# Products of zeros between stretches of 32x32 products, in a delta-rule attention with two MLPs behind it

## The chip, the cores and the metric

The kernel runs on one core of a Trainium2 chip. The metric is device time in microseconds (us); the median of three runs of the kernel before stands below.

## The reference

The reference is a gated delta-rule attention over 32 heads (4 batches of 8) of 768 positions and 48 dimensions, followed by two MLPs over 3072 tokens of 384 channels, each with 2048 hidden channels. Cut to what matters:

```python
k_n = k / (norm(k) + 1e-6)
state = zeros((B, H, D, D))
for t in range(S):
    y[:, :, t] = q[:, :, t] @ state
    v_old = state @ k_n[:, :, t]
    state = state + beta[:, :, t] * outer(k_n[:, :, t], v[:, :, t] - v_old)
x = y.transpose(0, 2, 1, 3).reshape(3072, 384)
h = x @ w_in;  x = (P(h) / Q(h)) @ w_out        # first MLP, a rational function
h = x @ w_in2; out = (h * tanh(softplus(h))) @ w_out2   # second MLP
```

## The kernel before, in words

The attention comes first and takes some 320 us; the MLPs follow. The attention works on 12 chunks of 64 positions (u = 0 to 11), all 32 heads at once, as 16 pairs in two halves (h = 0, 1). `Plan.add` records each operation with an engine, an assumed duration in ns, and the buffers it reads and writes; `Plan.best` tries 800 orders of the list and keeps the one whose planned end is earliest; `Plan.run` then emits the operations in that planned order. So each engine has a fixed queue, and in it the work of several chunks is interleaved.

For each chunk, `prepare` normalizes the keys (GpSimd), transposes keys and queries on TensorE (`kn`, `qn`, the products of line 352), copies them out on ScalarE (`kq`), forms the 64x64 gram matrices (line 367) and masks them on VectorE (`gm`, `lg`, line 376). For every second chunk, `inverse` solves a 32x32 triangular system per head step by step on GpSimd (on VectorE for u = 1 and u = 9); its result, transposed on VectorE at line 464, is `xt`, which two chunks share. `step` is the recurrence. For each half h of a chunk it does on TensorE, with 16 products in each group:

- `ks` (line 511): keys by the state `su`, 64x64 weights, 48 columns, into `c_ps`; VectorE subtracts (`rest`, line 519, into `r`)
- `uu` (line 528): `xt` by the remainder, 32x32 weights, 48 columns; ScalarE copies out `u` (line 535)
- `cross` (line 543): the lower block's correction, 32x32 weights, 48 columns; VectorE subtracts
- `uu` again, for the lower 32 rows, and the copy of `u`
- `s_mm` (line 551): the new state in `s_all`, copied out by ScalarE (line 559), which the next chunk's `ks` reads
- `y_mm` (line 566): the outputs in `y_ps`, 64 columns, copied out by ScalarE (line 575)

All of these are float32, so the trace shows two matmul records for each product: a group of 16 products of one half is x32, both halves are x64.

Beside this the plan holds the conversion of the first MLP's weights: loads on the SP queue, a magnitude on ScalarE (line 667), bit operations on VectorE (lines 672 to 688), a copy on ScalarE (line 698) and a difference on GpSimd (line 703).

`heat` is one product of zeros: a 128x128 tile `zero` with 128 columns of the identity, added to columns of PSUM that no one reads (`y_ps` at first, later columns 384 to 511 of `s_all`). `Plan.run` puts such products where the plan has a gap on TensorE, as many as fill 0.9 of it at 200 ns each, less up to 600 ns of idle time. Sixteen more stand at the start. The MLP phase has none.

Of the kernel before, what the change touches and what calls it, by code (L numbers as in the profile page):

```python
# [45 lines left out]
class Ring:  # L46
# [6 lines left out]
    def add(self, pool, **bufs):  # L53
        for tag, b in bufs.items():
            slots = self.slots.setdefault(tag, [])
            self.n[tag] = len(slots)
            slots.extend((pool, b) for _ in range(b))
# [8 lines left out]
class Plan:  # L66
# [12 lines left out]
        self.read = {}  # L79
        self.names = []  # L80

    def add(self, engine, ns, fn, reads=(), writes=(), more=0, early=0):
        i = len(self.ops)
        need = {self.wrote[b] for b in reads if b in self.wrote}
        for b in writes:
            need.update(self.read.pop(b, ()))
            if b in self.wrote:
                need.add(self.wrote[b])
        for b in reads:
            self.read.setdefault(b, []).append(i)  # L90
        for b in writes:
            self.wrote[b] = i
        self.names.append(tuple(writes))
        self.ops.append((engine, ns, fn, sorted(need), more, early))

    def order(self, bias=None):

        n = len(self.ops)
        tail, then, left = [0] * n, [[] for _ in range(n)], [0] * n
        for i in range(n - 1, -1, -1):  # L100
            engine, ns, fn, need, more, early = self.ops[i]
            tail[i] += ns + more
            left[i] = len(need)
            for j in need:
                then[j].append(i)
                tail[j] = max(tail[j], tail[i] + self.HOP)
        tail = [t - self.ops[i][5] + (bias or {}).get(self.kinds[i], 0) for i, t in enumerate(tail)]
        ready = {}
        for i in range(n):
            if not left[i]:  # L110
                ready.setdefault(self.ops[i][0], []).append((0, i))
        free, at, done = {}, [0] * n, []
        while any(ready.values()):
            best = None
            for engine, queue in ready.items():
                if queue:
                    t = max(free.get(engine, 0), min(r for r, _ in queue))
                    if best is None or t < best[0]:
                        best = (t, engine)
            t, engine = best  # L120
            queue = ready[engine]
            pick = max((x for x in queue if x[0] <= t), key=lambda x: (tail[x[1]], -x[1]))
            queue.remove(pick)
            i = pick[1]
            end = t + self.ops[i][1]
            free[engine] = end
            done.append((t, end, i))
            for j in then[i]:
                left[j] -= 1
                at[j] = max(at[j], end + self.ops[i][4] + (0 if self.ops[j][0] == engine else self.HOP))  # L130
                if not left[j]:
                    ready.setdefault(self.ops[j][0], []).append((at[j], j))
        return done
# [3 lines left out]
    def best(self):  # L137

        def end(order):
            return max(e for _, e, _ in order)  # L140
        self.kinds = [(op[0], names[0].strip("0123456789") if names else "") for op, names in zip(self.ops, self.names)]
        kinds, rng = sorted(set(self.kinds)), random.Random(0)
        bias, order = {}, self.order()
        for _ in range(self.TRIALS):
            trial = dict(bias)
            for k in rng.sample(kinds, rng.choice((1, 2, 4))):
                trial[k] = trial.get(k, 0) + rng.gauss(0, rng.choice((1000, 5000, 20000)))
            other = self.order(trial)
            if end(other) <= end(order):
                bias, order = trial, other  # L150
        return order

    WINDOW, IDLE = 3400, 600

    def run(self, idle, unit):

        last, gaps, used = None, [], False
        for t, end, i in self.best():
            engine, ns, fn = self.ops[i][:3]
            if engine == "PE":  # L160
                if last is not None and t > last:
                    gone = sum(max(0, b - max(a, last - self.WINDOW)) for a, b in gaps[-8:])
                    n = max(0, int((t - last - max(0, self.IDLE - gone)) * 0.9 // unit))
                    for _ in range(n):
                        idle(used)
                    gaps.append((last + n * unit, t))
                last, used = end, used or "y_ps" in self.names[i]
            fn()


class Attention:
# [311 lines left out]
    def step(self, p, u):  # L483
# [5 lines left out]
        gm, gmb = self.gm[u % self.NT], f"gm{u % self.NT}"  # L489
        v, vb = self.v[u % self.NV], f"v{u % self.NV}"  # L490
# [4 lines left out]
        i = self.side(u)  # L495
        xt, xb = self.xt[i], f"xt{i}"
        r2, y_ps = self.r2, self.y_ps
        yst, yb = self.yst[0], "yst"

        def each(h):  # L500
            for n in range(W):
                for a in range(2):
                    yield n, a, 64 * (a ^ h), slice(64 * a, 64 * a + 64)

        def out(h, rows, n):
            return self.c_ps[h][rows, n * D:(n + 1) * D]

        def ks(h):
            def f():
                for n, a, r, rows in each(h):  # L510
                    nc.tensor.matmul(  # L511
                        out=out(h, rows, n), lhsT=kq[r:r + 64, 0, n, rows],
                        rhs=S[r:r + 64, h, n, :], start=True, stop=True,
                    )
            return f

        def rest(h, src):
            part = slice(W * h, W * h + W)
            return lambda: nc.vector.tensor_tensor(
                out=r2[:, part], in0=src[:, part],  # L520
                in1=self.c_ps[h][:, 0:W * D].rearrange("p (m d) -> p m d", m=W), op=ALU.subtract,
            )

        def uu(h, c):
            def f():
                for n, a, r, rows in each(h):
                    rows = slice(64 * a + HC * c, 64 * a + HC * c + HC)
                    nc.tensor.matmul(  # L528
                        out=out(h, rows, n), lhsT=xt[rows, u % 2 * M + W * h + n, :], rhs=(r2 if u or c else v)[rows, W * h + n, :],
                        start=True, stop=True,  # L530
                    )
            return f

        def u_out(h):
            return lambda: nc.scalar.copy(
                out=U[:, W * h:W * h + W].rearrange("p m d -> p (m d)"), in_=self.c_ps[h][:, 0:W * D]
            )

        def cross(h):
            def f():  # L540
                for n, a, r, rows in each(h):
                    src, dst = slice(64 * a, 64 * a + HC), slice(64 * a + HC, 64 * a + C)
                    nc.tensor.matmul(
                        out=out(h, dst, n), lhsT=gm[src, W * h + n, 0:HC], rhs=U[src, W * h + n, :], start=True, stop=True,
                    )
            return f
# [32 lines left out]
        def y_add(h, part):  # L579
            need = [f"{ub}{h}", f"{gmb}{2 * h}", f"{gmb}{2 * h + 1}"] if part else [f"{sb}{h}", f"{kqb}1{0}", f"{kqb}1{1}"]  # L580
            if u or part:
                p.add("PE", 1080, y_mm(h, part), need, ["y_ps"])

        p.add("SP", LOAD, lambda: self.load_v(v, u), (), [vb], more=1800)
        for h in range(2):
            c, s, r, uh = f"c{h}", f"{sb}{h}", f"r{h}", f"{ub}{h}"
            if h:
                y_add(1, 0)
            if u:
                p.add("PE", 900, ks(h), [f"{kqb}00", f"{kqb}01", s], [c])  # L590
                p.add("DVE", 560, rest(h, v), [c, vb], [r])
            p.add("PE", 860, uu(h, 0), [r if u else vb, xb], [c])
            p.add("ACT", 480, u_out(h), [c], [uh])
            p.add("PE", 860, cross(h), [f"{gmb}{2 * h}", f"{gmb}{2 * h + 1}", uh], [c])
            p.add("DVE", 560, rest(h, r2 if u else v), [c] if u else [c, vb], [r])
            p.add("PE", 860, uu(h, 1), [r, xb, "y_ps"] if h else [r, xb], [c])
            p.add("ACT", 480, u_out(h), [c], [uh])
        if u + 1 < self.NU:
            for h in range(2):
# [361 lines left out]
def tile_delta_attention_two_mlps(  # L961
# [120 lines left out]
    with ExitStack() as bctx:  # L1082
# [24 lines left out]
        for i in range(n2 + max(LG.values())):  # L1107
# [8 lines left out]
            for op in LISTS[kind]:  # L1116
# [5 lines left out]
                elif op[0] == "u" and i < n2:  # L1122
                    if i not in ups:
                        ups[i] = mlp(i).up(i, *units[i])
                    n = int(op[1])
                    run(ups[i][3 * n:3 * n + 3])
                elif op[0] in "dvy" and 0 <= i - LAG - (op[0] == "y") < n2:
                    j = i - LAG - (op[0] == "y")
# [59 lines left out]
```

## Time and profile before

| | |
|---|---|
| median of 3 runs | 1160.14 us (1158.69 to 1165.7) |
| the profiled execution | 1162.92 us, of which the span from first to last instruction is 1161.2 us |
| attention | from the start to about 321.9 us of the span |
| TensorE busy | 1085.8 us, 94% of the span |
| mean granted TensorE clock | 0.960 of full speed |

The granted clock is a share of 2.4 GHz: 1.00 is 2.4 GHz and 0.50 is 1.2 GHz. In a timeline, the columns are the start, the time to the end of the piece, engine, line, operation and tiles with the shape of the weights and of the columns, how many, and in brackets the idle time of the engine before it with what ended it. "issue" there means that the engine waited for nothing that the profile shows. In a table of windows, "(x...)" is the number of records.

### The profile page before, as it was taken

To read this page: it belongs to the slowest core of one execution; us is meant where nothing else is said; L and a number is where in the kernel's file an instruction comes from. 1 tells how busy PE (TensorE), PEld (TensorE's weight loads), DVE (VectorE), ACT (ScalarE), POOL (GpSimd) and SP (SyncE) were. 2 spreads that over 40 slices of the span, in tenths; PEclk is the share of its full clock that TensorE was granted. 3 is DMA by queue.
4 is the path that set the end of the run, shared out by engine and by line. 5 is a ranking of instruction groups with operands and counts; after the bars stand their busy time and mean duration, and the time that the engine had idled before them with its cause. 6 is when DMAs were issued, how large, how long until landed. Compare 5 with 4: busy or idle time off the path is not lost.

```text
span 1161.2 us, 25029 instructions
## 1 busy us (share of the span) xinstructions
PE 1085.8 (94%) x10354; PEld 945.9 (81%) x10354; DVE 722.5 (62%) x1214; ACT 612.1 (53%) x1093; POOL 532.8 (46%) x607
## 2 busy tenths in 40 slices
PE   5989999878869898999999999999999999999998
PEld 4888888778858777877778778679999999999997
DVE  5976574995658999899898999886121221212110
ACT  4425445323468787888888888754332223333322
POOL 3187877477247676677777767783000000000000
PEclk9998798988889998999999999999999999999999
DMA  7437576226693020120212022161100001010000
GB/s 142 82 83 191 139 209 143 80 58 193 180 351 125 21 96 21 48 68 21 76 41 75 21 69 89 34 210 57 55 1 23 33 1 55 1 55 1 28 1 28
DMA packets 122418, 92.95 MB, mean 80 GB/s; under 512 B 79936, under 2 KB 106688, under 8 KB 122304
## 3 DMA queue, kind: packets, MB, share of 16 engines
q1 hardware_dynamic: 122048, 91.25, 26.9%
q8 instruction: 81, 1.33, 0.5%
q14 instruction: 33, 0.27, 0.1%
q0 software_dynamic: 256, 0.10, 0.1%
HBM read 63.02 MB, written 28.31 MB: 79 GB/s over the span
## 4 chain that ended last, share of the span: by engine, by line
PE 50%; DVE 14%; POOL 14%; ACT 13%; issue 8%; DMA 1%; POOLq 0%; DVEq 0%; ACTq 0%; SPq 0%
PE h L831 19%; PE o L950 17%; POOL q L874 8%; ACT r L881 3%; POOL r L864 3%; ACT q L861 2%; PE c_ps L528 2%; POOL gh L846 2%; ACT r L883 2%; PE y_ps L566 2%; PE c_ps L511 2%; PE o L917 2%; PE s_all L551 2%; DVE tmp L451 2%; DVE gm L376 1%
## 5 line engine op out<-in xcount | busy, mean ns | idle before, releaser
L831 PE MATMUL h<-x,w 128*128 128x512 f32 x1728 | 436.0, 397 | 23.5 <-DVE s L890 13.1
L831 PEld LDWEIGHTS h<-x,w 128*128 128x128 f32 x1728 | 324.3, 190 | 97.6 <-DVE s L890 27.5
L846 DVE TENSOR_TENSOR gh<-g,gh 128x512 fp32r<-128x512 f32 x88 | 63.3, 720 | 286.8 <-ACT g L941 286.8
L950 PE MATMUL o<-w,gh 128*128 128x384 f32 x1152 | 217.5, 337 | 2.0 <-ACT ev L1039 2.0
L917 PE MATMUL o<-gh,w 128*128 128x512 f32 x864 | 214.3, 392 | 0.4 <-ACT ev L1039 0.3
L950 PEld LDWEIGHTS o<-w,gh 128*128 128x128 f32 x1152 | 204.5, 188 | 10.8 <-ACT ev L1039 2.7
L917 PEld LDWEIGHTS o<-gh,w 128*128 128x128 f32 x864 | 163.3, 189 | 36.3 <-ACT ev L1039 2.1
L936 ACT ACTIVATE gh<-h 128x512 fp32r<-128x512 f32 x96 | 57.6, 600 | 215.0 <-PE h L831 215.0
L874 POOL TENSOR_TENSOR q<-q,r 128x512 f32<-128x512 f32 x96 | 127.5, 1328 | 81.6 <-ACT r L868 77.1
L846 POOL TENSOR_TENSOR gh<-g,gh 128x512 fp32r<-128x512 f32 x104 | 136.9, 1316 | 10.9 <-ACT g L941 6.9
L881 ACT ACTIVATE r<-q,cst 128x512 f32<-128x512 f32 x96 | 66.4, 692 | 60.5 <-POOL q L874 60.5
L703 POOL TENSOR_TENSOR w<-wm,w 128x384 fp32r<-128x384 f32 x48 | 48.9, 1020 | 74.7 <-ACT w L698 74.0
L897 DVE SCALAR_TENSOR_TENSOR q<-q,r 128x512 f32<-128x512 f32 x96 | 65.6, 683 | 27.7 <-ACT r L883 27.1
L870 ACT ACTIVATE s<-h,ab 128x512 f32<-128x512 f32 x96 | 74.4, 775 | 0.0
L890 DVE SCALAR_TENSOR_TENSOR s<-s,ab,h 128x512 f32<-128x512 f32 x96 | 71.8, 748 | 3.4
L901 DVE SCALAR_TENSOR_TENSOR r<-s,ab,r 128x512 f32<-128x512 f32 x96 | 71.8, 748 | 0.0
L888 DVE TENSOR_TENSOR s<-s,h 128x512 f32<-128x512 f32 x96 | 65.4, 681 | 9.9 <-ACT s L870 9.9
L906 DVE SCALAR_TENSOR_TENSOR g<-q,r 128x512 f32<-128x512 f32 x96 | 65.9, 687 | 3.3
L457 POOL TENSOR_TENSOR xs<-xs,tmp 128x30 f32<-128x30 f32 (+14 forms) x120 | 62.3, 519 | 9.4
L861 ACT ACTIVATE q<-h 128x512 f32<-128x512 f32 x96 | 57.2, 595 | 13.2 <-PE h L831 13.2
L864 POOL TENSOR_SCALAR r<-q,ab 128x512 f32<-128x512 f32 x54 | 43.4, 803 | 42.6 <-ACT q L861 42.6
L451 POOL TENSOR_TENSOR tmp<-xs 128x30 f32<-128x30 f32 (+14 forms) x120 | 58.6, 488 | 7.0
(125 smaller groups left out, 1403.7 us busy)
## 6 DMA issues: line engine op xcount, KB each, us to landing
w<-w SPq DMA_DIRECT2D x28, 768.0 KB, 7.5
w<-in_moe_w_in_dram SPq DMA_DIRECT2D x32, 384.0 KB, 3.8
w<-in_moe_w_out_dram SPq DMA_DIRECT2D x32, 384.0 KB, 3.5
xraw<-x SPq DMA_DIRECT2D x36, 256.0 KB, 3.9
kn<-in_k_dram SPq DMA_DIRECT2D x48, 96.0 KB, 3.4
qn<-in_q_dram SPq DMA_DIRECT2D x48, 96.0 KB, 3.2
v<-in_v_dram SPq DMA_DIRECT2D x48, 96.0 KB, 3.2
x<-yst SPq DMA_DIRECT2D x24, 192.0 KB, 3.8
```

The costliest lines, as they stand in the source:

```text
L451: eng.tensor_tensor(out=tv, in0=ls[:, j, j + 1:HC].unsqueeze(1).to_broadcast([128, j, n]), in1=xs[:, 0:j, j:j + 1].to_broadcast([128, j, n ...
L831: self.nc.tensor.matmul(out=self.st[i]["h"], lhsT=self.w.t[f][:, a, 0, k], rhs=self.x[g][:, b, k], start=(n == 0), stop=(n == 8),)
L846: (nc.gpsimd if engine == "P" else nc.vector).tensor_tensor(out=s["gh"][:, 1], in0=s["g"], in1=s["gh"][:, 0].bitcast(F32), op=ALU.subtract)
L861: nc.scalar.activation(out=s["q"], in_=s["h"], func=ACTF.Abs)
L864: nc.gpsimd.tensor_scalar(out=s["r"], in0=s["q"], scalar1=k["b1"], scalar2=k["b0"], op0=ALU.mult, op1=ALU.add)
L870: nc.scalar.activation(out=s["s"], in_=s["h"], func=ACTF.Identity, scale=k["a3"], bias=k["a2"])
L874: nc.gpsimd.tensor_tensor(out=s["q"], in0=s["q"], in1=s["r"], op=ALU.mult)
L881: nc.scalar.activation(out=s["r"], in_=s["q"], func=ACTF.Ln, bias=k["c"])
L890: nc.vector.scalar_tensor_tensor(out=s["s"], in0=s["s"], scalar=k["a1"], in1=s["h"], op0=ALU.add, op1=ALU.mult)
L901: nc.vector.scalar_tensor_tensor(out=s["r"], in0=s["s"], scalar=k["a0"], in1=s["r"], op0=ALU.add, op1=ALU.mult)
L917: self.nc.tensor.matmul(out=self.acc[g][d], lhsT=self.w.t[f][:, a, 1, d], rhs=self.st[i]["gh"][:, b], start=(first and n == 0), stop=(last ...
L950: self.nc.tensor.matmul(out=self.acc[g][t][:, 0:384], lhsT=self.st[i]["gh"][:, a, t * 128:(t + 1) * 128], rhs=self.w.t[f][:, b, 1].rearran ...
```

## The change

`Plan.add` gets a flag `small`, which is set on the operations `uu` and `cross`. `Plan.run` now keeps a list `work` of the last TensorE operations with a weight: 0.4 for a small one, 1.0 for any other and for the products of zeros. Before every TensorE operation, whether the plan has a gap there or not, it sums the weighted work of the plan's last 3400 ns (over the last 16 entries) and adds up to three products of zeros, as many 200 ns products as are missing to 0.7 of that time.

```diff
-    WINDOW, IDLE = 3400, 600
+    WINDOW, IDLE, ACTIVE = 3400, 600, 0.7
...
-        last, gaps, used = None, [], False
+        last, gaps, work, used = None, [], [], False
         for t, end, i in self.best():
-            engine, ns, fn = self.ops[i][:3]
+            engine, ns, fn, small = *self.ops[i][:3], self.ops[i][6]
             if engine == "PE":
-                if last is not None and t > last:
+                if last is not None:
                     gone = sum(max(0, b - max(a, last - self.WINDOW)) for a, b in gaps[-8:])
                     n = max(0, int((t - last - max(0, self.IDLE - gone)) * 0.9 // unit))
+                    done = n * unit + sum(w * max(0, b - max(a, t - self.WINDOW)) for a, b, w in work[-16:])
+                    n += max(0, min(3, round((self.ACTIVE * self.WINDOW - done) / unit)))
                     for _ in range(n):
                         idle(used)
-                    gaps.append((last + n * unit, t))
+                    if t > last:
+                        gaps.append((min(t, last + n * unit), t))
+                    work.append((t - n * unit, t, 1.0))
+                work.append((t, end, 0.4 if small else 1.0))
                 last, used = end, used or "y_ps" in self.names[i]
             fn()
...
-            p.add("PE", 860, uu(h, 0), [r if u else vb, xb], [c])
+            p.add("PE", 860, uu(h, 0), [r if u else vb, xb], [c], small=True)
...
-            p.add("PE", 860, cross(h), [f"{gmb}{2 * h}", f"{gmb}{2 * h + 1}", uh], [c])
+            p.add("PE", 860, cross(h), [f"{gmb}{2 * h}", f"{gmb}{2 * h + 1}", uh], [c], small=True)
...
-            p.add("PE", 860, uu(h, 1), [r, xb, "y_ps"] if h else [r, xb], [c])
+            p.add("PE", 860, uu(h, 1), [r, xb, "y_ps"] if h else [r, xb], [c], small=True)
```

On TensorE's queue the kernel has 233 products of zeros before and 297 after, 64 more. The order of all other work on TensorE is as it was, and so is that of VectorE, GpSimd and the SP queue; on ScalarE one copy of the first chunk's `kq` stands one place later. Line numbers of the kernel after are higher by 5.

Chunk 4 on TensorE, where `xt` has just come ready: two transposes, then `uu`, `cross` and `uu` of both halves (`c_ps_168` and `c_ps_169`) and `s_mm`. Before:

```order
L1059 MATMUL s_all_167<-ident_119,zero 128x128 x31
L352 MATMUL t_ps_171<-ident_119,kn_124 128x128 x4
L352 MATMUL t_ps_170<-ident_119,kn_124 128x128 x4
L528 MATMUL c_ps_169<-r_146,xt_152 32x48 x16
L528 MATMUL c_ps_168<-r_146,xt_152 32x48 x16
L543 MATMUL c_ps_169<-u_145,gm_141 32x48 x16
L543 MATMUL c_ps_168<-u_145,gm_141 32x48 x16
L528 MATMUL c_ps_169<-r_146,xt_152 32x48 x16
L528 MATMUL c_ps_168<-r_146,xt_152 32x48 x16
L551 MATMUL s_all_167<-u_145,kn_126 48x48 x32
```

The same place in the kernel after, from the first `uu`:

```order
L533 MATMUL c_ps_169<-r_146,xt_152 32x48 x16
L533 MATMUL c_ps_168<-r_146,xt_152 32x48 x16
L548 MATMUL c_ps_169<-u_145,gm_141 32x48 x16
L1064 MATMUL s_all_167<-ident_119,zero 128x128 x3
L548 MATMUL c_ps_168<-u_145,gm_141 32x48 x16
L1064 MATMUL s_all_167<-ident_119,zero 128x128 x2
L533 MATMUL c_ps_169<-r_146,xt_152 32x48 x16
L533 MATMUL c_ps_168<-r_146,xt_152 32x48 x16
L556 MATMUL s_all_167<-u_145,kn_126 48x48 x16
L1064 MATMUL s_all_167<-ident_119,zero 128x128
L556 MATMUL s_all_167<-u_145,kn_126 48x48 x16
```

Three, two and one products of zeros now stand inside the run of 32x32 products and in `s_mm`; chunk 10 has the same three groups at the same places.

Chunk 2 on TensorE, where `uu` and `cross` are mixed with output products (`y_ps`). Before:

```order
L528 MATMUL c_ps_169<-r_146,xt_151 32x48 x16
L566 MATMUL y_ps_172<-kq_133,su_143 48x64 x16
L528 MATMUL c_ps_168<-r_146,xt_151 32x48 x16
L543 MATMUL c_ps_169<-u_145,gm_139 32x48 x16
L543 MATMUL c_ps_168<-u_145,gm_139 32x48 x16
L528 MATMUL c_ps_169<-r_146,xt_151 32x48 x16
L528 MATMUL c_ps_168<-r_146,xt_151 32x48 x16
```

After:

```order
L533 MATMUL c_ps_169<-r_146,xt_151 32x48 x16
L571 MATMUL y_ps_172<-kq_133,su_143 48x64 x16
L533 MATMUL c_ps_168<-r_146,xt_151 32x48 x16
L548 MATMUL c_ps_169<-u_145,gm_139 32x48 x16
L1064 MATMUL s_all_167<-ident_119,zero 128x128 x2
L548 MATMUL c_ps_168<-u_145,gm_139 32x48 x16
L1064 MATMUL s_all_167<-ident_119,zero 128x128
L533 MATMUL c_ps_169<-r_146,xt_151 32x48 x16
L1064 MATMUL s_all_167<-ident_119,zero 128x128 x2
L533 MATMUL c_ps_168<-r_146,xt_151 32x48 x16
```

Five products of zeros came in here, in three groups. Over the whole attention there are 30 new groups: 10 of three, 13 of two and 7 of one; one old group grew from 8 to 10 and another shrank from 2 to 1. By chunk, the added products are 5 ahead of chunk 0 (between the first transposes), then 6, 2, 5, 5, 6, 2, 4, 6, 5, 6, 6 and 6 for chunks 0 to 11 (chunks overlap on the queue; a group between two of them is counted with the later).

## Rows read from the trace of the kernel before

**Rows 1.** The page's chain of work that ended last, by engine: shares of the span.

```profile
PE 50%; DVE 14%; POOL 14%; ACT 13%; issue 8%; DMA 1%; POOLq 0%; DVEq 0%; ACTq 0%; SPq 0%
```

**Rows 2.** Windows: the stretches of the attention whose granted clock is low (PEclk).

```profile
core 0: us, PE busy (x) PEld busy (x) DVE busy (x) ACT busy (x) POOL busy (x), PEclk, DMA share, GB/s
86.30:96.54 10.24, 10.24 (x143) 9.25 (x144) 4.12 (x9) 4.44 (x9) 6.66 (x12) 0.50 0.72 207
117.02:123.85 6.83, 6.83 (x175) 6.71 (x172) 5.60 (x12) 4.01 (x11) 5.52 (x9) 0.50 0.73 223
130.68:140.92 10.24, 9.62 (x211) 8.94 (x206) 3.62 (x7) 3.87 (x8) 7.71 (x12) 0.50 0.33 75
171.64:185.29 13.65, 13.05 (x262) 12.31 (x260) 3.35 (x6) 3.45 (x8) 9.13 (x17) 0.50 0.64 164
216.01:219.42 3.41, 3.38 (x36) 2.96 (x35) 3.24 (x12) 0.01 (x1) 2.94 (x7) 0.50 0.00 0
239.90:246.73 6.83, 6.83 (x142) 6.36 (x138) 5.90 (x12) 1.00 (x3) 5.97 (x12) 0.50 0.02 6
263.80:274.04 10.24, 10.16 (x234) 9.78 (x234) 4.59 (x9) 2.97 (x8) 6.56 (x10) 0.50 0.77 225
297.93:308.17 10.24, 9.22 (x218) 8.94 (x218) 5.59 (x10) 4.77 (x10) 2.00 (x2) 0.50 0.64 200
```

**Rows 3.** Timeline of PE: `uu` and `s_mm` of both halves, first at clock 0.50, then 1.00.

```profile
135.28 2.77 PE L528 MATMUL c_ps<-r,xt 32*32 32x48 f32 x64
137.98 2.52 PE L551 MATMUL s_all<-u,kn 64*48 64x48 f32 x64
...
282.27 1.55 PE L528 MATMUL c_ps<-r,xt 32*32 32x48 f32 x64
283.77 1.55 PE L551 MATMUL s_all<-u,kn 64*48 64x48 f32 x64
```

**Rows 4.** Timeline of PE: groups of products of zeros, each with the product behind it.

```profile
209.02 0.61 PE L1059 MATMUL s_all<-ident,zero 128*128 128x128 f32 x4
209.55 0.66 PE L352 MATMUL t_ps<-ident,qn 128*128 128x128 f32 x4
...
231.94 0.71 PE L1059 MATMUL s_all<-ident,zero 128*128 128x128 f32 x4
232.59 0.92 PE L551 MATMUL s_all<-u,kn 64*48 64x48 f32 x32
...
292.49 0.94 PE L1059 MATMUL s_all<-ident,zero 128*128 128x128 f32 x6
293.36 1.10 PE L566 MATMUL y_ps<-kq,su 64*48 64x64 f32 x32
```

**Rows 5.** Timeline of PE: what stands last before five falls of the clock.

```profile
86.30 1.22 PE L367 MATMUL t_ps<-kq 64*64 64x128 f32 x17 [1.90 <-issue]
...
115.88 0.95 PE L543 MATMUL c_ps<-u,gm 32*32 32x48 f32 x34 [1.07 <-issue]
...
168.60 1.55 PE L543 MATMUL c_ps<-u,gm 32*32 32x48 f32 x64 [0.70 <-ACT u L535]
...
261.43 1.55 PE L528 MATMUL c_ps<-r,xt 32*32 32x48 f32 x64 [2.32 <-DVE r L519]
...
296.21 1.55 PE L543 MATMUL c_ps<-u,gm 32*32 32x48 f32 x64 [0.28 <-ACT u L535]
```

**Rows 6.** Groups of PE from 0 to 335 us: busy, mean ns, idle before, releasers.

```profile
L566 PE MATMUL y_ps<-kq,su 64*48 64x64 f32 x704 | 25.8, 227 | 2.1 <-ACT yst L575 2.1
L551 PE MATMUL s_all<-u,kn 64*48 64x48 f32 x704 | 24.1, 243 | 2.3 <-ACT u L535 1.2 <-issue 1.0
L543 PE MATMUL c_ps<-u,gm 32*32 32x48 f32 x768 | 22.7, 212 | 5.1 <-ACT u L535 2.8 <-issue 2.1
```

**Rows 7.** Timelines of POOL and DVE: two places where the triangular solve meets the queue.

```profile
153.00 1.00 POOL L703 TENSOR_TENSOR w<-wm,w 128x384 fp32r<-128x384 f32 x1 [5.38 <-ACT w L698]
...
286.81 1.91 POOL L461 TENSOR_TENSOR xs<-xs,beta 128x1024 f32<-128x1024 f32 x1
...
292.08 2.11 DVE L464 STREAM_TRANSPOSE xt<-xs 128x1024 f32<-128x1024 f32 x1
```

More of the change, by code (lines that the diff above doesn't have):

```diff
@@ L80, in __init__, with add @@
         self.names = []
-    def add(self, engine, ns, fn, reads=(), writes=(), more=0, early=0):
+    def add(self, engine, ns, fn, reads=(), writes=(), more=0, early=0, small=False):
         i = len(self.ops)
@@ L93, in add @@
         self.names.append(tuple(writes))
-        self.ops.append((engine, ns, fn, sorted(need), more, early))
+        self.ops.append((engine, ns, fn, sorted(need), more, early, small))
     def order(self, bias=None):
@@ L100, in order @@
         for i in range(n - 1, -1, -1):
-            engine, ns, fn, need, more, early = self.ops[i]
+            engine, ns, fn, need, more, early, _ = self.ops[i]
             tail[i] += ns + more
```

## The prediction

> **What bounds the kernel now.** I read the chain of waits first: TensorE (PE) holds half of it [rows 1], and the change touches its queue in the attention alone, some 320 us of 1161. So the question is what limits that stretch. The windows come next. The granted clock there falls to 0.50, which is 1.2 of 2.4 GHz, in eight stretches [rows 2]; the reader is to see that PE is busy nearly throughout them, so they are not idle time. They add up to 71.7 us. Third, the timeline gives the price of such a stretch: the same 64 records of `uu` take 2.77 us at 0.50 and 1.55 at 1.00, `s_mm` 2.52 and 1.55 [rows 3], factors of 1.79 and 1.63, on average 1.7. If PE alone sets the pace, a low stretch of length L would shrink by L x (1 - 1/1.7) = 0.41 L.
>
> PE doesn't set it everywhere. From 216 to 220 and from 240 to 247 us VectorE is busy for 3.24 of 3.41 and 5.90 of 6.83 us with the solve of chunk 9 [rows 2]; I count nothing for these two. The other six are 61.4 us long and are worth at most 0.41 x 61.4 = 25.2 us.
>
> Fourth, what stands before the falls [rows 5]. The one at 171.64 follows 64 records each of `uu`, `cross` and `uu` with 0.70 us of idle time among them, the one at 297.93 a like run with 0.28 us. There PE was at work, but only on 32x32 products. Before 117.02 a run of 32x32 products has a hole of 1.07 us in which PE waits for its own next instructions ("issue"); 130.68 is the same pattern one chunk later. Before 86.30 there is a hole of 1.90 us, and before 263.80 one of 2.32 us, in which PE waits for VectorE.
>
> **The change part by part.** *The price of the products of zeros.* Two of them between `uu` and `s_mm` push `s_mm` from 231.94 to 232.59, 0.65 us; three push `y_mm` from 292.49 to 293.36, 0.87 us [rows 4]. The third costs 0.22 us, so I estimate one alone at 0.43. With 10 new groups of three, 13 of two, 7 of one and one product net in old groups: 8.7 + 8.45 + 3.0 + 0.2 = 20.4 us of PE time, at full clock.
>
> Two products between transposes, which are 128x128 as they are, take only 0.53 us [rows 4]. The Trainium skill (TensorEngine Tiling (Array Packing), Key Properties) says that a change of tiling mode drains the engine, and a group among 32x32 products makes two such changes; the trace agrees as far as 0.65 against 0.53 goes. Without that the groups would come to some 17 us.
>
> *What hides them.* The groups of chunks 6 and 7 (3.0 us) fall into the solve on VectorE from 225 to 260 us; PE waits for VectorE there, and I count 2.0 us as hidden. If that cover were gone they would cost the full 3.0. PE's idle time directly ahead of `cross`, `s_mm` and the `y_mm` of keys and queries is 5.1 + 2.3 + 2.1 = 9.5 us over the attention [rows 6], some of it waits for ScalarE's copies and some holes in its own instructions. The new groups stand ahead of about half of it, and a group only hides up to the length of the wait: 5.4 us. This leaves 20.4 - 2.0 - 5.4 = 13.0 us on the path. The ends are 20.4 - 3.0 - 9.5 = 7.9 and 20.4.
>
> *What is queued behind them.* The copies on ScalarE and the subtractions on VectorE wait for the products behind a group, and in the same queues stand the weight conversion and, behind it, GpSimd's solve. So a delay of PE passes on: GpSimd sits 5.38 us behind a copy of weights at 153 us [rows 7]. The five products ahead of chunk 0 delay the first transposes and with them the first solve, by about 1 us, which is in the sum. No other queue is moved, and ScalarE's one exchanged copy costs nothing, as PE's product is late either way. The MLP phase has no such products and only starts earlier or later.
>
> *What they buy.* For each fall a chance that it doesn't come, by what now stands before it, times its worth of 0.41 L. 171.64 (13.65 us long, worth 5.6): six products of zeros within the run, 0.85. 297.93 (10.24, worth 4.2): the same six, 0.7, as that run was the denser. 117.02 (2.8) and 130.68 (4.2): five each, but the hole of 1.07 us may stay, 0.5. 86.30 (4.2): nothing was added close to the hole; it may move, 0.35. 263.80 (4.2): its cause stays, five products come in the low stretch and may shorten it, 0.4. Sum: 4.8 + 2.9 + 1.4 + 2.1 + 1.5 + 1.7 = 14.4 us. Every later piece stands at another time, so a fall can also come where there was none: one of 9 us, at 0.41 and a chance of 0.6, takes 2.2 back. 12.2 us are left.
>
> *What is late next.* A faster PE meets the solve. `xt` for chunk 10 starts on VectorE at 292.08; GpSimd's solve for it ends at 286.81 + 1.91 = 288.72 [rows 7], so at most 3.4 us can be won there. The two falls of chunks 2 and 3 end in GpSimd's wait of 5.38 us, and can't give more than that. I take 1.2 us off: 11.0.
>
> *Sum.* 13.0 - 11.0 = 2.0 us slower. The profiled execution took 1162.92 us, 1.7 of them outside the span, 2.8 above the median; on the median the sum makes 1160.1 + 2.0 = 1162.
>
> **The rivals.** *The clock doesn't follow the zeros* (slower). If falls come from idle time only, then products inside busy runs avert none. Against it: 297.93 falls with 0.28 us of idle time in the run before it; for it: four of the six falls do have a hole of 1 to 2.3 us ahead of them [rows 5]. Then the 13.0 us stand alone, and five products in a low stretch cost 0.7 times more, 1 us: 1160 + 14 = 1174. It decides as soon as less than 3 us of low clock disappear; from 13.0 / 0.41 = 32 us on, the products pay.
>
> The Trainium skill (TensorE: Matmul & The Clock Gate, table "Why this matters for your kernels") names idle gaps between bursts as what drops throughput, and its loop advice is to keep products back to back. Taken alone this would make 1174 the likeliest; the fall at 297.93 behind a busy run speaks against it here.
>
> *All six falls go* (faster). For it: the two densest runs get six products each, and a run with 32x32 products mixed with others kept its clock at 1.00, as at 282.27 [rows 3]. Against it: three of the holes aren't touched. It gives 25.2, less 1.6 that the 5.38 us cap takes of the 7.0 of chunks 2 and 3, less 0.8 at chunk 10: 22.8 - 13.0 = 9.8 us, 1150; with all 9.5 us of idle time as cover it is 1146.
>
> *It doesn't do what it says.* The queue shows all 64 products, so this can only be the first rival.
>
> **How the numbers follow.** About 1% (11.6 us) is what a measurement of this kernel can tell from no change. The forecast, part of the falls gone, has 0.73, from 1152 (two falls more than I count, at 4 us each, and 2 us more hidden) to 1171 (two fewer, and 1 us less hidden). The first rival has 0.15, the second 0.12, of which some 0.08 lie under 1148.5. Slower by over 1% is the first rival with a little less than its whole chance, 0.14, and 0.02 of the forecast's tail; faster by over 1% gets 0.10 with a tail of the forecast. The range from 1147 to 1175 takes in both rivals' times and leaves the ends out.
>
> **What would show it.** In the trace after: the windows of the attention should show three to five low stretches instead of eight, 35 to 45 us in place of 71.7; none at the `uu`, `cross`, `uu` run of chunk 4; groups of two in 0.65 us and of three in 0.87; PE's first product of the MLP within some 10 us of where it was. I am wrong if the low stretches are as many as before (the first rival), if a group costs far less because PE would have waited anyway (then the sum is a gain of up to 10 us), or if a shifted instruction hole drops the clock at new places.

## The result, and the profile after

The kernel after took 1166.53 us (median of 20 runs, 1157.75 to 1175.25), the kernel before beside it 1158.9 us (20 runs, 1147.09 to 1168.88): a ratio of 1.0084 [1.0056, 1.0111]. The ratio compares the means of the fast runs, those within 1.5% of each kernel's fastest; over all runs the means differ by 8.6 us. The forecast was 1162; the change costs some 8 us where it said 2. That is under the 1% bound of the prediction, but with this many runs it is told from no change.

The profiled execution took 1166.23 us, 3.3 more than that of before. First the page's chain, by engine, which answers to [rows 1]:

```profile
PE 53%; POOL 14%; ACT 12%; DVE 12%; issue 8%; DMA 1%; SPq 0%; POOLq 0%; DVEq 0%; ACTq 0%
```

TensorE's share of the chain rose from 50 to 53%. By line, first before and then after, the products of zeros into `s_all` (line 1064) are new on the page's list:

```profile
PE h L831 19%; PE o L950 17%; POOL q L874 8%; ACT r L881 3%; POOL r L864 3%; ACT q L861 2%; PE c_ps L528 2%; POOL gh L846 2%; ACT r L883 2%; PE y_ps L566 2%; PE c_ps L511 2%; PE o L917 2%; PE s_all L551 2%; DVE tmp L451 2%; DVE gm L376 1%
PE h L836 19%; PE o L955 17%; POOL q L879 8%; ACT r L886 3%; PE c_ps L533 3%; POOL r L869 3%; ACT q L866 2%; PE y_ps L571 2%; POOL gh L851 2%; ACT r L888 2%; PE s_all L1064 2%; PE o L922 2%; PE c_ps L548 2%; DVE tmp L456 1%; PE c_ps L516 1%
```

So products of zeros did land on the path. The windows of the attention's low stretches (columns as in [rows 2]):

```profile
74.44:84.68 10.24, 10.24 (x166) 9.45 (x159) 4.85 (x9) 2.95 (x6) 3.55 (x6) 0.50 0.36 90
118.81:129.05 10.24, 10.24 (x212) 9.44 (x210) 5.53 (x12) 5.27 (x12) 7.93 (x13) 0.50 0.72 209
207.56:210.97 3.41, 3.41 (x30) 3.19 (x32) 3.30 (x4) 1.51 (x3) 3.25 (x4) 0.50 0.61 102
238.28:248.52 10.24, 10.00 (x168) 9.22 (x168) 6.56 (x13) 0.96 (x2) 8.93 (x17) 0.50 0.01 2
sum 34.13, PE 33.89 PEld 31.30 DVE 20.24 ACT 10.68 POOL 23.67; mean PE 8.47 PEld 7.82 DVE 5.06 ACT 2.67 POOL 5.92
```

Four stretches of 34.1 us stand where [rows 2] has eight of 71.7. The falls at 130.68, 171.64, 263.80 and 297.93 have no counterpart; those at 117.02, 216.01 and 239.90 have one within 9 us. The one at 86.30 is gone too, and the one at 74.44 is new. Next, the timeline of TensorE at the run of chunk 4, where the clock of before fell at 171.64:

```profile
168.42 0.87 PE L548 MATMUL c_ps<-u,gm 32*32 32x48 f32 x32
169.22 0.94 PE L1064 MATMUL s_all<-ident,zero 128*128 128x128 f32 x6
170.09 0.87 PE L548 MATMUL c_ps<-u,gm 32*32 32x48 f32 x32
170.88 0.71 PE L1064 MATMUL s_all<-ident,zero 128*128 128x128 f32 x4
171.53 1.55 PE L533 MATMUL c_ps<-r,xt 32*32 32x48 f32 x64
173.00 0.92 PE L556 MATMUL s_all<-u,kn 64*48 64x48 f32 x32
173.85 0.49 PE L1064 MATMUL s_all<-ident,zero 128*128 128x128 f32 x2
174.28 0.92 PE L556 MATMUL s_all<-u,kn 64*48 64x48 f32 x32
```

From start to start, three products take 0.87 us (169.22 to 170.09), two 0.65 (170.88 to 171.53) and one 0.43 (173.85 to 174.28): the unit prices are as forecast from [rows 4]. `uu` takes 1.55 us, so the clock is at 2.4 GHz here.

The holes at or ahead of the four falls of this kernel, in the timeline of TensorE:

```profile
73.92 2.11 PE L533 MATMUL c_ps<-v,xt 32*32 32x48 f32 x58 [1.75 <-DVE xt L469]
...
116.92 0.78 PE L548 MATMUL c_ps<-u,gm 32*32 32x48 f32 x28 [1.46 <-issue]
...
205.48 1.09 PE L357 MATMUL t_ps<-ident,kn 128*128 128x128 f32 x8 [1.39 <-POOL kn L401]
...
238.52 1.49 PE L533 MATMUL c_ps<-r,xt 32*32 32x48 f32 x32 [1.34 <-DVE r L524]
```

Each is 1.3 to 1.8 us long, and the products don't fill it. The first hole isn't new: the kernel before waited 1.8 us for that `xt` too, but its clock fell only at 86.30. Inside the low stretch from 74.44 on, the products themselves cost more, 1.58 us for three (77.18 to 78.76):

```profile
77.18 1.65 PE L1064 MATMUL y_ps<-ident,zero 128*128 128x128 f32 x6
78.76 1.49 PE L548 MATMUL c_ps<-u,gm 32*32 32x48 f32 x32
```

Last, the groups of TensorE over the attention, which answer to [rows 6], and those of the products of zeros (`s_all` only: those into `y_ps` went from 38.5 to 44.1 us):

```profile
L1064 PE MATMUL s_all<-ident,zero 128*128 128x128 f32 x264 | 42.4, 302 | 1.1 <-issue 1.0
...
L571 PE MATMUL y_ps<-kq,su 64*48 64x64 f32 x704 | 24.1, 218 | 1.6 <-ACT yst L580 1.6
L548 PE MATMUL c_ps<-u,gm 32*32 32x48 f32 x768 | 23.3, 213 | 4.1 <-issue 2.4 <-ACT u L540 1.7
L556 PE MATMUL s_all<-u,kn 64*48 64x48 f32 x704 | 21.0, 217 | 1.1 <-issue 0.9 <-ACT u L540 0.2
```

The idle time ahead of these three is 6.8 us, where [rows 6] has 9.5. Added up over all groups of TensorE up to its first product of the MLP, the ledger of the two traces is: products of zeros 59.6 to 86.5 us (+26.9), other work 243.8 to 226.5 (-17.3, the work that now runs at the higher clock), idle time 45.2 to 41.8 (-3.4). Busy times of neighbouring groups overlap, so these add up to more than the 4.1 us by which the attention is longer. That product starts at 326.0 instead of 321.9 us:

```profile
326.01 4.38 PE L836 MATMUL h<-x,w 128*128 128x512 f32 x18 [0.91 <-DVE wm L693]
```

**Reading all runs, not one trace.** Each run lists its span and its mean granted clock, and (1 - clock) x 2 x span is the time that it spent at 0.50, "low clock" below. It counts the whole kernel; the MLP phase and rounding add some 8 to 25 us to what the attention's windows show. In 75 runs of the kernel before, those beside the experiments, it goes from 50 to 110 us, mean 75.8, and time follows it. (The 20 runs of before above have no clock on record; their mean time is 1158.0 us, that of the 75 is 1158.4.) One line for each kernel, with a common slope fitted to the 197 runs (75 of before, 20 of after, 6 or 12 of each other kernel), gives 0.331 +- 0.011 us of time for each us of low clock; the times scatter about the lines by 2.1 us. The height of a kernel's line is its time if the clock never fell; its distance from before's line is the price of a change, with the clock taken out.

| kernel | products added | low clock, mean us | price, us | worth of the change in low clock, us |
|---|---|---|---|---|
| before | 0 | 75.8 | 0 | 0 |
| after | 64 | 53.7 | 15.5 | -7.3 |
| e1_less | 14 | 65.1 | 1.7 | -3.5 |
| e2_more | 138 | 33.6 | 27.7 | -14.0 |
| e3_rows32 | 64, of 32 rows | 86.8 | 12.5 | +3.6 |
| e4_late | 53 | 67.9 | 15.2 | -2.6 |
| e5_waits | 42, in gaps | 71.3 | 5.6 | -1.5 |
| e6_none | -79, in gaps | 121.5 | -3.9 | +15.1 |
| e7_runs | 25 | 68.4 | 6.4 | -2.5 |
| e8_bf16 | 64, bfloat16 | 72.2 | 5.2 | -1.2 |
| e9_early | 11 | 72.3 | 0.9 | -1.2 |
| e10_early_less | 19 | 71.5 | 3.9 | -1.4 |

Prices are good to 1 to 2 us and the means of low clock to some 4 us, which is 1.4 us of worth. For the kernel after, 15.5 - 7.3 = 8.2 us is the difference between its mean and that of the 75 runs; the table divides it into price and return and doesn't prove it a second time. A trial outside the fit is the profiled execution of before, which isn't among the 75: from it to the profiled execution of after, low clock falls from 92.9 to 55.9 us, worth 37.0 x 0.331 = 12.2 us, and 15.5 - 12.2 = 3.3 us is what the two times differ by.

### The profile page after: what moved, and what is told of

Its sections match the earlier page's. It is cut to its first block, busy times and chain, and to the rows that moved or that the text cites. A ratio compares the mean times of both kernels' runs of the same rounds, so it can differ in the third digit from the quotient of the medians.

```text
span 1164.5 us, 25284 instructions
## 1 busy us (share of the span) xinstructions
PE 1093.5 (94%) x10482; PEld 949.9 (82%) x10482; DVE 720.0 (62%) x1214; ACT 611.7 (53%) x1093; POOL 531.6 (46%) x607
## 3 DMA queue, kind: packets, MB, share of 16 engines
q1 hardware_dynamic: 122048, 91.25, 26.9%
q8 instruction: 82, 1.34, 0.5%
## 4 chain that ended last, share of the span: by engine, by line
PE 53%; POOL 14%; ACT 12%; DVE 12%; issue 8%; DMA 1%; SPq 0%; POOLq 0%; DVEq 0%; ACTq 0%
PE h L836 19%; PE o L955 17%; POOL q L879 8%; ACT r L886 3%; PE c_ps L533 3%; POOL r L869 3%; ACT q L866 2%; PE y_ps L571 2%; POOL gh L851 2%; ACT r L888 2%; PE s_all L1064 2%; PE o L922 2%; PE c_ps L548 2%; DVE tmp L456 1%; PE c_ps L516 1%
## 5 line engine op out<-in xcount | busy, mean ns | idle before, releaser
L895 DVE SCALAR_TENSOR_TENSOR s<-s,ab,h 128x512 f32<-128x512 f32 x96 | 71.7, 747 | 3.4
```

Of the source, the lines that this page charges most:

```text
L895: nc.vector.scalar_tensor_tensor(out=s["s"], in0=s["s"], scalar=k["a1"], in1=s["h"], op0=ALU.add, op1=ALU.mult)
```

## The experiments

The experiments ran in three groups on three chips (e1 to e4, e5 to e8, e9 and e10), each beside its own runs of before, whose medians are 1157.39, 1157.04 and 1158.09 us; with the clock taken out, before differs by some 1 us between the three. The times are medians of 6 or 12 runs.

**e1_less: a lower share, 14 products.**

```diff
-    WINDOW, IDLE, ACTIVE = 3400, 600, 0.7
+    WINDOW, IDLE, ACTIVE = 3400, 600, 0.5
```

> The plan asks for 0.5 of its last 3400 ns instead of 0.7: 14 products of zeros are added instead of 64, in six groups (three ahead of chunk 0, three in chunk 0, two each within the 32x32 runs of chunks 2, 4, 8 and 10). Price theory (each added product costs 0.3 to 0.4 us of TensorE time, little of it hidden, and a clock that stays up gives back less than that): the groups cost some 5 us, and at least the dense runs of chunks 4 and 10 keep their clock, which is worth 4 to 8 us; time 1156 to 1160, low stretches 35 to 55 us in all. Rival, the clock doesn't follow the zeros: low stretches as before, near 70 us, and the time 1159 + 5 = 1164.

Measured: 1156.01 us, ratio 0.9989 [0.9957, 1.0022]. It can't be told from before. The price of 1.7 us and the return of 3.5 in the table differ by no more than their errors.

**e2_more: a higher share, 138 products.**

```diff
-    WINDOW, IDLE, ACTIVE = 3400, 600, 0.7
+    WINDOW, IDLE, ACTIVE = 3400, 600, 0.85
```

> The plan asks for 0.85 instead of 0.7: 138 products of zeros are added in 61 new groups, 74 more than in the changed kernel. Price theory: another 20 to 25 us of TensorE time, while only the 34 us of low clock that are left can go (some 10 us at most): 1166 + 12 = 1175 to 1190. Rival, the zeros are hidden in waits and the loss of the changed kernel is chance or new waits for instructions: no slower than the changed kernel, 1160 to 1168.

Measured: 1172.85 us, ratio 1.0135 [1.0091, 1.0178]. Its windows of low clock in the attention:

```profile
207.00:210.42 3.42, 3.37 (x16) 3.37 (x16) 3.31 (x4) 2.17 (x5) 3.19 (x5) 0.50 0.83 155
254.79:258.20 3.41, 3.41 (x84) 3.41 (x84) 3.27 (x7) 0.49 (x2) 1.43 (x3) 0.50 0.26 56
312.82:316.23 3.41, 3.41 (x46) 3.07 (x42) 1.47 (x3) 1.07 (x3) 1.00 (x1) 0.50 0.55 202
```

Only 10.2 us are left in this execution, which has the least low clock of the six (23.3 us over the whole kernel; the others have 35 to 38). The kernel is slower than the one after: its 74 further products add 27.7 - 15.5 = 12.2 us of price and 14.0 - 7.3 = 6.7 of return. That price is about half of the 20 to 25 us expected, so the time stayed below the range of 1175 to 1190.

**e3_rows32: the added products fill a quarter of the array.** They have the same columns and the same places, but 32 of 128 rows of weights and columns.

```diff
+                    for _ in range(extra):
+                        idle(used, 32)
...
-                out=at.s_ps[1][:, DM:DM + 128] if used else at.y_ps[:, 0:128], lhsT=zero, rhs=at.ident,
+                out=at.s_ps[1][:, DM:DM + 128] if used else at.y_ps[:, 0:128], lhsT=zero[0:rows], rhs=at.ident[0:rows],
```

> The 64 added products of zeros stand where they stand in the changed kernel, with as many columns and instructions, but fill 32 of the array's 128 rows. If the granted clock follows how much of the array is filled, the price stays and the return goes: low stretches 55 to 75 us, time 1172 to 1182. If it follows columns or busy time alone: low stretches near 34 us and the time of the changed kernel, 1166. If the zeros never moved the clock: also 1166, but with low stretches of any length.

Measured: 1175.86 us, ratio 1.0148 [1.0107, 1.019]. The timeline at chunk 4 of this kernel, and the window that begins in it:

```profile
171.05 0.87 PE L551 MATMUL c_ps<-u,gm 32*32 32x48 f32 x32 [1.14 <-ACT u L543]
171.85 0.93 PE L1067 MATMUL s_all<-ident,zero 32*128 32x128 f32 x6
172.71 0.87 PE L551 MATMUL c_ps<-u,gm 32*32 32x48 f32 x32
173.50 0.71 PE L1067 MATMUL s_all<-ident,zero 32*128 32x128 f32 x4
174.14 2.51 PE L536 MATMUL c_ps<-r,xt 32*32 32x48 f32 x64
```

```profile
174.48:191.55 17.07, 16.47 (x320) 15.33 (x316) 3.35 (x6) 4.28 (x9) 8.43 (x15) 0.50 0.50 126
```

The groups take the same 0.86 and 0.64 us as with 128 rows, and the clock falls behind them, where the kernel after keeps it. That one place isn't proof by itself, as the run has an idle 1.14 us ahead of it here. The runs are: low clock is 77 to 96 us in all six, against 28 to 82 in the twenty of the kernel after. The return is gone, the price (12.5 us) stays. The mean of 86.8 us is even above the 75.8 of before; no run shows why.

**e4_late and e9_early: the two halves of the change.** e4_late leaves out the 11 products ahead of chunk 1, e9_early has only these (`if not used:`).

```diff
-                    n += max(0, min(3, round((self.ACTIVE * self.WINDOW - done) / unit)))
+                    if used:
+                        n += max(0, min(3, round((self.ACTIVE * self.WINDOW - done) / unit)))
```

> The 11 products of zeros that the change adds ahead of chunk 1 (five between the first transposes, six in chunk 0) are left out, the other 53 stay. Price theory: these 11 are on the path of the first solve and of chunk 0 with nothing to hide them, so 2 to 4 us less than the changed kernel, 1163. Rival, the start is hidden behind the solve of the second pair: no difference, 1166.

Measured: 1170.25 us, ratio 1.0086 [1.0043, 1.0128]. Leaving the early products out gained nothing, and both times expected were missed: the price is that of the kernel after (15.2 and 15.5 us), but there is more low clock. That raised the question whether they alone are a gain:

> Of the change's 64 products of zeros only the 11 ahead of chunk 1 (five between the first transposes, six in chunk 0). Against the changed kernel, the kernel without these 11 had the same time at equal clock and 14 us more low clock. If that is theirs: price about 0, 8 to 14 us less low clock than before at 0.33 each, so 3 to 5 us faster than before, 1152 to 1155. Rival, that difference was the scatter of where the falls come, and each product costs its 0.2 us: 1157 to 1160.

Measured: 1158.57 us, ratio 1.0008 [0.9978, 1.0039]. The gain expected isn't there, and the time is the rival's. They cost 0.9 us in the table and return 1.2, neither beyond its error. The price of the change is that of the 53 later ones, 15.2 us.

**e5_waits: more products only where the plan has a gap.** The kernel before with 42 more of its own kind.

```diff
-    WINDOW, IDLE = 3400, 600
+    WINDOW, IDLE = 3400, 0
```

> The kernel before, with one number changed: gaps of the plan are filled from their first ns on (600 ns are left idle before), so 42 products of zeros are added where the plan has TensorE wait, and none elsewhere. Theory of cover (the price of a product is what stands of it outside a wait): price 0 to 4 us, some 15 us less low clock than before at 0.34 us each, so 1151 to 1157. Rival, every added product costs the 0.24 us that those of the change cost at equal clock: price 10 us, return 5 us, 1162 to 1165.

Measured: 1163.23 us, ratio 1.0039 [1.0006, 1.0072]. The theory of cover missed, and the time is the rival's. Even in the plan's gaps a product costs 5.6 / 42 = 0.13 us, about half of the rival's 0.24, and the 42 return only 1.5 us. A gap of the plan need not be one on the chip; the runs don't show whether that is the reason.

**e6_none: the kernel before without its 79 products behind the first output product.**

```diff
-                    for _ in range(n):
+                    for _ in range(0 if used else n):
```

> The kernel before without the 79 products of zeros that it has behind the first output products. Theory of cover: they stand in waits and cost next to nothing, and without them the clock is low for 30 us more, so 1157 + 0.34 x 30 = 1165 to 1172. Rival, their own price is as large as what they return: 1155 to 1161.

Measured: 1168.75 us, ratio 1.0105 [1.0064, 1.0146], as the theory of cover expected. The longest of its windows of low clock:

```profile
154.74:171.80 17.06, 11.56 (x264) 11.04 (x264) 12.33 (x18) 6.67 (x13) 15.44 (x27) 0.50 0.54 178
202.52:219.59 17.07, 13.24 (x121) 9.95 (x120) 16.44 (x32) 6.84 (x13) 10.91 (x18) 0.50 0.24 56
...
294.68:325.40 30.72, 27.69 (x569) 25.99 (x564) 15.20 (x28) 9.75 (x22) 4.98 (x5) 0.50 0.38 125
```

TensorE has long idle times in the first two (11.56 and 13.24 us busy of 17), so the products that stood there had time to hide in. All 79 together cost almost nothing, 3.9 / 79 = 0.05 us each, and kept off 45.7 / 79 = 0.58 us of low clock each. The old products pay for themselves several times over; the new ones stand where little such idle time is.

**e7_runs: products only within the dense runs**, where the last three operations of TensorE were small; 25 are added.

```diff
-                    n += max(0, min(3, round((self.ACTIVE * self.WINDOW - done) / unit)))
+                    if [x[2] for x in work if x[1] > x[0]][-3:] == [0.4] * 3:
+                        n += max(0, min(3, round((self.ACTIVE * self.WINDOW - done) / unit)))
```

> The change's rule is asked only where the last three TensorE operations of the plan were all of 32x32 products: 25 products of zeros are added instead of 64. If the return comes from the dense runs (chunks 4, 8, 10), low clock is 12 to 20 us less than before, worth 4 to 7 us, at a price of 3 to 6: 1154 to 1158, the changed kernel's loss gone. Rival, the return is spread evenly over all products (0.37 us of low clock each): 9 us less low clock and 3 back, 1158 to 1161.

Measured: 1162.31 us, ratio 1.0029 [0.9993, 1.0065]. Both ranges expected were missed. It pays 6.4 us and gets 2.5 back: the runs in which [rows 5] shows falls without a hole are not a better place by themselves.

**e8_bf16: the same 64 products in bfloat16.** One record each.

```diff
+                    for _ in range(extra):
+                        idle(used, True)
...
-                out=at.s_ps[1][:, DM:DM + 128] if used else at.y_ps[:, 0:128], lhsT=zero, rhs=at.ident,
+                out=at.s_ps[1][:, DM:DM + 128] if used else at.y_ps[:, 0:128], lhsT=zero16 if half else zero, rhs=ident16 if half else at.ident,
```

> The 64 added products of zeros are bfloat16 (zeros by a bfloat16 identity) instead of float32, one record each instead of two, at the same places. Price at equal clock: half or less, 5 to 8 us in place of 15. Return: if it goes by the time that the array is filled, half, 12 us of low clock and 4 us of time, so 1159 to 1162; if a group of short products keeps the clock as well as one of long products, 8 us return and 1155 to 1158.

Measured: 1162.3 us, ratio 1.0052 [1.0023, 1.0082]. Its timeline between the first transposes, in chunk 2 and in chunk 10, at the higher clock up to the last line shown, in which it falls:

```profile
17.64 0.33 PE L1071 MATMUL y_ps<-ident,zero 128*128 128x128 bf16 x3
17.80 0.61 PE L360 MATMUL t_ps<-ident,kn 128*128 128x128 f32 x4
...
117.79 0.23 PE L1071 MATMUL s_all<-ident,zero 128*128 128x128 bf16 x1
117.95 0.87 PE L536 MATMUL c_ps<-r,xt 32*32 32x48 f32 x32
...
296.52 0.34 PE L1071 MATMUL s_all<-ident,zero 128*128 128x128 bf16 x3
296.79 0.87 PE L551 MATMUL c_ps<-u,gm 32*32 32x48 f32 x32
297.59 0.28 PE L1071 MATMUL s_all<-ident,zero 128*128 128x128 bf16 x2
297.81 1.80 PE L536 MATMUL c_ps<-r,xt 32*32 32x48 f32 x64
```

The first transposes in the kernel after, with three float32 products:

```profile
17.54 0.83 PE L1064 MATMUL y_ps<-ident,zero 128*128 128x128 f32 x6
18.21 0.60 PE L357 MATMUL t_ps<-ident,kn 128*128 128x128 f32 x4
```

Among 32x32 products, from start to start, a group takes 0.16 us with one product, 0.22 with two and 0.27 with three: some 0.055 for each product and a fixed part of 0.11. The float32 groups (0.43, 0.65, 0.87) have 0.22 for each product and a fixed part of 0.21. Between transposes, which are 128x128 too, three products take 0.16 and 0.67 us (float32), so there no fixed part is left. Ten groups at 0.27, 13 at 0.22 and 7 at 0.16 are 6.7 us, the price in the table is 5.2, as expected. Of the return half was expected, and it is almost gone: low clock is 72.2 us, against 75.8 before. These products are shorter and have half as many records; which of the two took the return isn't shown.

The Trainium skill (TensorEngine Tiling (Array Packing), Key Properties) says that a change of tiling mode drains the engine and gives no price; these rows agree, with a fixed 0.21 us in float32 and 0.11 in bfloat16 for the two changes of a group, and none where the tiling stays.

**e10_early_less: the early products as they are, and the lower share behind them**, 19 products, as the best guess at a version faster than both.

```diff
-                    n += max(0, min(3, round((self.ACTIVE * self.WINDOW - done) / unit)))
+                    n += max(0, min(3, round(((0.5 if used else self.ACTIVE) * self.WINDOW - done) / unit)))
```

> The 11 products ahead of chunk 1, and from there on the rule with 0.5 in place of 0.7: 8 more, two each in the 32x32 runs of chunks 2, 4, 8 and 10, 19 in all. If few products in the densest places return 0.8 us of low clock each, as with 14 of them, at 0.1 us each: 15 us less low clock, 5 us back for 2, 1153 to 1156, the fastest of all. Rival, the price is 0.24 each and the return 0.35: 1159 to 1161.

Measured: 1159.79 us, ratio 1.0023 [0.9989, 1.0057]. No gain: the time is the rival's. No version beats before by more than its interval.

## Why the prediction came near, point by point

**The mechanism held.** The products keep the clock up, part of the falls goes, and the price is on TensorE's path. The dose shows it: with 79 fewer, 0, 64 and 138 more products the low clock is 121.5, 75.8, 53.7 and 33.6 us. The first rival, that the clock doesn't follow the zeros, falls: e3_rows32 has the columns and the places of the change and groups as long, without its filling, and its low clock is 33 us higher. The second, that all six falls go, would have made a gain. The change doesn't do it, and e2_more, which comes nearest to it in the clock, needs 138 products for it and still loses.

The Trainium skill (TensorE: Matmul & The Clock Gate, table "Why this matters for your kernels") names idle gaps between bursts as what drops throughput in mid-kernel. The traces agree in part. The falls that are left have holes of 1.34 to 1.75 us at or ahead of them, but these are shorter than the gaps that the table warns of, and the kernel before fell at 171.64 and 297.93 behind busy runs with 0.70 and 0.28 us of idle time [rows 5]. In e3_rows32 the added products differ from those of the change only in the rows that they fill, and low clock is 33 us more.

**The falls.** Those at 171.64 and 297.93, with chances of 0.85 and 0.7, are gone, and so are 130.68 (0.5) and 263.80 (0.4). Of those with a hole, 117.02 (0.5) stayed as 118.81. The one at 86.30 (0.35) is gone, and the new fall that the sum allowed for (0.6) came at 74.44. Forecast were three to five low stretches of 35 to 45 us; there are 4 of 34.1, and the first product of the MLP is 4.1 us late, within 10. There is luck in this: it compares one execution of each kernel, and that of before was a bad one. Over all runs the drop is 22.1 us, not 37.

**Where the sum was off: the return.** The prediction took 11.0 us; the runs show 7.3. Two steps carry that. *"They add up to 71.7 us"* is true of one execution, which was an unlucky one: by its clock of 0.960 its low clock is 92.9 us over the whole kernel, where the mean of 75 runs is 75.8 and only 9 of them have as much. So there was some 17 us less to win than [rows 2] shows, and the drop over all runs is 22.1 us, where the forecast of 12.2 us at 0.41 meant 30. *"0.41 L"* was the ratio of TensorE's own times at the two clocks [rows 3]; the fitted worth is 0.33. At 0.41 the 22.1 us would be worth 9.1: of the 12.2 us ahead of the cap, 3.1 go with the first step and 1.8 with the second, in which the cap of 1.2 is contained. That other engines set the pace in a part of each stretch would make the worth smaller; this was argued from windows like 239.90 in [rows 2] and not isolated.

**And the price.** 20.4 us gross holds by its unit prices. The part on the path is 15.5, not 13.0. *"a group only hides up to the length of the wait: 5.4 us"* is the step, as far as one trace shows it: the idle time ahead of `cross`, `s_mm` and `y_mm` shrank by 9.5 - 6.8 = 2.7 us, and 20.4 - 2.0 - 2.7 = 15.7. In the other direction, the products ahead of chunk 0, counted at some 1 us, are in the 0.9 that all 11 early ones cost. The charge for zeros that run at 1.2 GHz (1.58 us for three, not 0.87) stood only in the rival, and was missing in the sum. Price and return erred the same way, by 2.5 and 3.7 us, which makes the 6 us between 2.0 and 8.2.

**What is late next.** `xt` for chunk 10 came at 294.87 instead of 292.08 [rows 7], 2.8 us later, while its solve ends at 287.29 + 1.91 = 289.20 instead of 288.72, 0.5 later. What held `xt` up is VectorE's queue ahead of it: the wait for a weight's magnitude from ScalarE ends at 290.44 instead of 286.33. Before:

```profile
286.33 0.56 DVE L672 TENSOR_SCALAR word<-wm 128x384 f32<-128x384 f32 x1 [3.83 <-ACT wm L667]
```

After:

```profile
287.29 1.91 POOL L466 TENSOR_TENSOR xs<-xs,beta 128x1024 f32<-128x1024 f32 x1
...
290.44 0.56 DVE L677 TENSOR_SCALAR word<-wm 128x384 f32<-128x384 f32 x1 [7.12 <-ACT wm L672]
...
294.87 2.12 DVE L469 STREAM_TRANSPOSE xt<-xs 128x1024 f32<-128x1024 f32 x1
```

GpSimd's wait behind a copy of weights, which the cap named, is shorter, 2.30 instead of 5.38 us, but it ends at 153.48 instead of 153.00:

```profile
153.48 1.00 POOL L708 TENSOR_TENSOR w<-wm,w 128x384 fp32r<-128x384 f32 x1 [2.30 <-ACT w L703]
```

So the 6.8 us less of low clock up to there (20.5 instead of 27.3) had gained nothing by this point: GpSimd itself came later, and the copy no sooner. Both places that the cap named are later than before, so in this pair the return was gone ahead of them and not held up by the solve. That the added products used it up is likely and not isolated: TensorE also had holes at new places, such as the one of 1.57 us at 287.41 shown below.

**What stays open.** Why the 53 late products return less without the 11 early ones (2.6 us in e4_late, 1.2 in e9_early, 7.3 together) is not settled: with errors of some 1.5 us on each, it may be scatter.

## What to carry to other kernels

A product that only keeps the clock up pays by what it returns less its price on the path: here 0.33 us of time for each us of low clock. In real idle time it costs 0.05 us and returns 0.58 us of low clock, 0.19 us of time. Between back-to-back products it costs 15.5 / 64 = 0.24 us and would have to return 0.24 / 0.331 = 0.73 us of low clock, while it returned 22.1 / 64 = 0.35. And before the low stretches of one profiled execution are taken as the budget, its mean clock should be held against that of many runs.

## What the runs showed that was not expected

- The same kernel spends from 50 to 110 us at the lower clock from run to run, and this alone spreads its times over some 20 us.
- How many rows the products of zeros fill makes the difference: with the same columns at the same places, products of 32 rows left a low clock of 86.8 us and products of 128 rows one of 53.7.
- A group of 128x128 products among 32x32 ones has a fixed cost, 0.21 us in float32 and 0.11 in bfloat16. Between 128x128 transposes it has none.
- Holes in which TensorE waits for its own instructions came at new places and grew, from 7.2 us in 8 pieces to 10.1 in 14 over the attention (counted from 60 us on). In the other traces they vary from 4.4 to 15.6 us, with no order that would tell a cause. One of the new ones, in the timeline of the kernel after:

```profile
287.41 0.53 PE L533 MATMUL c_ps<-r,xt 32*32 32x48 f32 x15 [1.57 <-issue]
```
